# A top-k attention stage: max and min of the score halves read one half in PSUM; TensorE instead of VectorE spreads the reciprocal row sums

## The chip, the core and the metric

The kernel runs on one core of a Trainium2 chip. The metric is device time in microseconds of one execution; the three runs of the kernel before gave 1383.68, 1383.35 and 1379.19 us, median 1383.35.

## The reference

Three stages follow each other. Attention has 4 batches, 8 heads, 576 rows and head dimension 64, and keeps in each row of scores only those that reach the 32nd largest:

```
scores = scale * q @ k.T
kth    = 32nd largest of each row
scores = where(scores >= kth, scores, -1e9);  scores -= row max
attn   = exp(scores);  attn /= sum(attn) + 1e-9;  out = attn @ v
```

Then every one of the 2304 tokens goes through `h = x @ w_in; g = h * cos(h); y = g @ w_out` (512 to 2048 to 512), and at last through one of eight experts (512 to 1024 to 512) that a gate picks by argmax, scaled by the gate and by a sigmoid.

## The kernel before, in words

The program describes each piece of work as an operation with an engine, an estimated duration, the buffers that it reads and writes and a priority. A planner (class Plan) then runs a list schedule: at each moment each engine takes the most urgent operation that can start, where a buffer's place must be free too. The instructions are issued in the order that comes out, and each engine executes its own queue strictly in that order. The estimates never appear on the chip; they only fix the order.

Attention is cut into 80 units: 64 "main" units (128 rows of queries, for two heads) and 16 "mixed" ones (the last 64 rows of two heads, stacked). Unit u has priorities around 10*u. One main unit does this:

- TensorE multiplies q by k: for each head j two matmuls of 288 columns, L551, into four PSUM banks (mixed units: L566). Head 0 stands on partitions 0 to 63 and head 1 on 64 to 127.
- ScalarE copies each of the four results from PSUM to the SBUF tile sc (L557, mixed L571), which frees the bank.
- VectorE takes the elementwise max ("up") and min ("dn") of the left and the right half of each row, L580: four instructions of 288 columns per main unit, two per mixed one, both inputs in SBUF. Rounds of MAX8 (L585, L590, L600) and MATCH_REPLACE8 (L595) then find the 32nd and 33rd largest.
- GpSimd turns the threshold into a bias (L604, L607, L609), ScalarE computes a mask from sc (L614), GpSimd subtracts it (L618), ScalarE takes the exponential with row sums (L621), GpSimd adds 1e-9 (L624).
- VectorE takes the reciprocal (L627) and then copies it, repeated over 64 columns per head, into a 128x128 tile rs (L629). TensorE transposes the weights (L641, L652) and rs (L653), ScalarE copies these out of PSUM (L644, L657), TensorE multiplies by v (L682), and VectorE scales the result by the transposed reciprocals (L688, mixed L692).

Scores have priority offset -13.9 and the max and min 4.5, so the scores of a unit are due almost two units ahead of its max and min.

Six of the eight PSUM banks are shared by everything that TensorE writes (tag "ps"): transposed q and k, scores, transposed weights, results, and the first matmul of the dense stage. The other two accumulate the dense stage's second matmul. In the trace all banks have the one name bank.

Beside attention the same queues carry the conversion of the float64 weights to two single-precision parts (VectorE L714, L716, L729; GpSimd L725, L727, L739, L749), and the dense stage for each two finished tiles of tokens (TensorE L765 to L767 and L816 to L818; VectorE L775, L795; GpSimd L773, L777, L808). Routing and the eight experts follow when attention is over. All this lies in one order per engine: whatever waits holds up what is queued behind it on its engine.

Of the kernel before, what the change touches and what calls it, by code (L numbers as in the profile page):

```python
# [14 lines left out]
OP = mybir.AluOpType  # L15
AX = mybir.AxisListType

P = 128
# [10 lines left out]
UP_POOL = 0  # L29
ADD = {'q': -10.1,  # L30
 's': -13.9,
# [23 lines left out]
 'rs': 1,  # L55
# [13 lines left out]
class Buf:  # L69
    """A value in one of the places of its tag; the place is picked when the first op starts."""  # L70
# [16 lines left out]
class Plan:  # L87
    """Orders the ops of all engines: takes them in program order, finds what depends on what,
    and gives each engine the most urgent op that can start."""
# [9 lines left out]
    def tag(self, name, places, loose=False, under=None):  # L99
        """`places`: (ap, area, first, last) each; `under`: tags whose last values must have left the place."""  # L100
# [154 lines left out]
def act(n, extra=0, psum=False):  # L255
    return (49.0 + n * 0.837 if psum else 92.0 + n * 0.836) + 93.0 * extra
# [11 lines left out]
def tile_topk_attention_moe_moe2(ctx, tc, q, k, v, w_in, w_out, w_gate, w_ogate, w1, w2, out):  # L268
# [68 lines left out]
    def x2_rows(j):  # L337
        kind, b, r = tiles[j]
        if kind == "m":
# [5 lines left out]
              + N["dn"] * HALF + N["bl"] * S + 9 * P + (N["qt"] + N["rs"] + N["xt"]) * P + 4 * (TOPK + 16) + 32  # L345
# [73 lines left out]
    cut.tag("rs", N["rs"], P)  # L419
# [6 lines left out]
    attn_tags = ("sc", "kt", "qr", "vr", "kr", "ptm", "ptx", "up", "dn", "bl", "qx", "vx", "kx", "qt", "rs", "xt", "mx",  # L426
# [99 lines left out]
    def attention(u):  # L526
# [18 lines left out]
        for c in range(2):  # L545
            if kind == "m":
                ps = [plan.buf("ps"), plan.buf("ps")]
                for j in range(2):
                    def mm(j=j, c=c, o=ps[j]):
                        at = (REM if j == 0 else 0) + c * HALF  # L550
                        nc.tensor.matmul(o.ap[:, 0:HALF], qt.ap[j * D:(j + 1) * D, :],  # L551
                                         kt.ap[j * D:(j + 1) * D, at:at + HALF], start=True, stop=True)

                    plan.op({"PE": 483.0}, mm, [qt, kt], [ps[j]], prio + ADD["s"], hold=[sc])
                for j in range(2):
                    plan.op({"ACT": act(HALF, psum=True)},
                            lambda j=j, c=c, o=ps[j]: nc.scalar.activation(  # L557
                                sc.ap[:, j, c * HALF:(c + 1) * HALF], o.ap[:, 0:HALF], AF.Copy),
                            [ps[j]], [(sc, j)], prio + ADD["s"])
            else:  # L560
                o = plan.buf("ps")

                def mm(c=c, o=o):
                    at = REM + c * HALF
                    for j in range(2):
                        nc.tensor.matmul(o.ap[j * D:(j + 1) * D, 0:HALF], qt.ap[j * D:(j + 1) * D, 0:REM],  # L566
                                         kt.ap[j * D:(j + 1) * D, at:at + HALF], start=True, stop=True)

                plan.op({"PE": 540.0}, mm, [qt, kt], [o], prio + ADD["s"], hold=[sc])
                plan.op({"ACT": act(HALF, psum=True)},  # L570
                        lambda c=c, o=o: nc.scalar.activation(sc.ap[:, 0, c * HALF:(c + 1) * HALF],  # L571
                                                              o.ap[:, 0:HALF], AF.Copy),
                        [o], [(sc, 0)], prio + ADD["s"])

# [814 lines left out]
```

## Time and profile before

| what | value |
|---|---|
| median of three runs | 1383.35 us |
| span of the profiled execution, first to last instruction | 1382.2 us |
| TensorE busy | 1180.1 us (85%) |
| VectorE busy | 988.5 us (72%) |
| GpSimd busy | 885.2 us (64%) |
| ScalarE busy | 854.9 us (62%) |

The profile lists no time of its own for the profiled execution beside its span of 1382.2 us, which is 1.2 us under the median of the runs. The shares are averages over stretches that differ: attention and the dense stage fill the first 1000 us, the end of the dense stage, routing and experts the rest. A group's busy time is the union of its instructions, which can overlap their neighbour by some 0.08 us; the mean, minimum and median durations count each whole. In the trace one single-precision matmul has two MATMUL records, a transpose has one, and a few records are missing.

### The profile page before, as it was taken

What the parts mean: (1) busy time and instruction counts of PE and PEld (TensorE: products, weight loads), DVE (VectorE), ACT (ScalarE), POOL (GpSimd) and SP (SyncE); (2) the same over time, 40 slices, a digit from 0 to 9 for tenths busy, and PEclk for the clock granted to TensorE, in tenths of its full rate; (3) what the DMA queues carried; (4) which work ended last, traced back from release to release, by engine and by line L of the source; (5) the groups of instructions that cost most, each with busy time, mean ns of one, the idle gap of its engine ahead of it and who ended that gap; (6) DMA issues with size and microseconds to landing.
All of it is one profiled execution on the core that took longest, in us unless ns stands there. A gap on an engine that the chain in (4) does not pass through costs nothing.

```text
span 1382.2 us, 22655 instructions
## 1 busy us (share of the span) xinstructions
PE 1180.1 (85%) x7478; PEld 936.6 (68%) x7479; DVE 988.5 (72%) x2864; ACT 854.9 (62%) x1854; POOL 885.2 (64%) x1130
## 2 busy tenths in 40 slices
PE   3467778768898999999989898899994599999996
PEld 2334555547677668668767676767883599999995
DVE  6999999779599888999987889888335234444410
ACT  5777777767577787777766668767555244444421
POOL 6778888888666865776676657766765455555400
PEclk9655779989999989999999999999996699999998
DMA  8223323534440343323345321241557444444100
GB/s 210 76 107 113 98 67 116 182 131 162 144 139 8 111 140 105 122 92 104 96 135 152 100 78 36 89 137 46 174 184 267 166 160 158 149 156 160 58 17 23
DMA packets 95807, 164.72 MB, mean 119 GB/s; under 512 B 49850, under 2 KB 54202, under 8 KB 95680
## 3 DMA queue, kind: packets, MB, share of 16 engines
q1 hardware_dynamic: 91264, 153.71, 34.3%
q0 software_dynamic: 4416, 9.47, 2.1%
q8 instruction: 61, 1.00, 0.3%
q14 instruction: 66, 0.54, 0.1%
HBM read 146.72 MB, written 19.56 MB: 120 GB/s over the span
## 4 chain that ended last, share of the span: by engine, by line
PE 41%; DVE 29%; POOL 13%; issue 10%; ACT 6%; DMA 2%; POOLq 0%; DVEq 0%; ACTq 0%
DVE area_a L590 7%; DVE area_a L595 6%; DVE area_a L580 6%; PE bank L682 4%; PE bank L551 3%; PE bank L816 3%; PE bank L818 3%; PE bank L817 3%; PE bank L1052 2%; PE bank L1053 2%; PE bank L641 2%; PE bank L1054 2%; POOL area_a L618 2%; PE bank L765 2%; POOL area_g L777 2%
## 5 line engine op out<-in xcount | busy, mean ns | idle before, releaser
L590 DVE MAX8 area_a<-area_a 128x8 f32<-128x288 f32 x576 | 243.6, 444 | 1.1
L618 POOL TENSOR_TENSOR area_a<-area_a 128x576 f32<-128x576 f32 x144 | 195.8, 1368 | 23.0 <-ACT area_a L614 21.9
L595 DVE MATCH_REPLACE8 area_a<-area_a 128x288 f32<-128x288 f32 x432 | 187.8, 438 | 0.0
L580 DVE TENSOR_TENSOR area_a<-area_a 128x288 f32<-128x288 f32 x288 | 176.7, 639 | 14.5 <-ACT area_a L557 11.0
L765 PE MATMUL bank<-area_f,area_w 128*128 128x256 f32 x576 | 177.6, 308 | 2.3 <-ACT area_h L771 2.3
L641 PE MATMUL bank<-ident,area_a 128*128 128x128 f32 x576 | 104.5, 313 | 70.6 <-ACT area_a L621 57.8
L766 PE MATMUL bank<-area_f,area_w 128*128 128x256 f32 x576 | 163.3, 284 | 0.0
L767 PE MATMUL bank<-area_f,area_w 128*128 128x256 f32 x576 | 163.0, 283 | 0.0
L551 PE MATMUL bank<-area_a 64*128 64x288 f32 x512 | 133.3, 513 | 25.5 <-ACT area_a L541 22.5
L641 PEld LDWEIGHTS bank<-ident,area_a 128*128 128x128 f32 x576 | 73.8, 158 | 100.3 <-ACT area_a L621 78.4
L816 PE MATMUL bank<-area_l,area_f 128*128 128x512 f32 x288 | 130.4, 453 | 1.3 <-ACT area_f L806 0.6
L614 ACT ACTIVATE area_a<-area_a 128x576 bf16<-128x576 f32 x144 | 107.3, 768 | 37.5 <-POOL area_a L604 37.2
L808 POOL TENSOR_TENSOR area_f<-area_g,area_f 128x256 fp32r<-128x256 f32 x144 | 114.9, 811 | 23.7 <-ACT area_f L806 20.8
L777 POOL TENSOR_TENSOR area_g<-area_g,area_n 128x512 f32<-128x512 f32 x72 | 105.7, 1468 | 35.3 <-DVE area_a L600 14.8
L621 ACT ACTIVATE area_a<-area_a 128x576 f32<-128x576 f32 x144 | 111.2, 773 | 27.1 <-POOL area_a L618 26.2
L682 PE MATMUL bank<-area_a 128*64 128x128 f32 (+3 forms) x1600 | 123.3, 296 | 1.5 <-ACT area_a L662 1.3
L818 PE MATMUL bank<-area_l,area_f 128*128 128x512 f32 x288 | 119.7, 416 | 5.3 <-POOL area_f L808 5.0
L765 PEld LDWEIGHTS bank<-area_f,area_w 128*128 128x128 f32 x576 | 112.1, 195 | 14.2 <-issue 9.2
L682 PEld LDWEIGHTS bank<-area_a 128*64 128x64 f32 (+1 forms) x1600 | 89.8, 150 | 42.3 <-issue 18.3
L817 PE MATMUL bank<-area_l,area_f 128*128 128x512 f32 x288 | 118.2, 410 | 0.0
L766 PEld LDWEIGHTS bank<-area_f,area_w 128*128 128x128 f32 x576 | 111.8, 194 | 1.0
L767 PEld LDWEIGHTS bank<-area_f,area_w 128*128 128x128 f32 x576 | 111.0, 193 | 0.0
(197 smaller groups left out, 3005.4 us busy)
## 6 DMA issues: line engine op xcount, KB each, us to landing
area_l<-wod SPq DMA_DIRECT2D x144, 512.0 KB, 3.6
area_l<-in_moe_w_dram SPq DMA_DIRECT2D x52, 512.0 KB, 4.3
area_l<-in_moe_w_in_dram SPq DMA_DIRECT2D x16, 512.0 KB, 4.3
area_l<-in_moe_w_out_dram SPq DMA_DIRECT2D x16, 512.0 KB, 4.1
wod<-area_l SPq DMA_DIRECT2D x16, 512.0 KB, 2.6
area_n<-in_moe_w_dram SPq DMA_DIRECT2D x12, 512.0 KB, 4.9
area_a<-in_k_dram SPq DMA_DIRECT2D x32, 128.0 KB, 3.5
area_a<-in_q_dram SPq DMA_DIRECT2D x32, 128.0 KB, 3.4
```

The source lines that it names most:

```text
L551: nc.tensor.matmul(o.ap[:, 0:HALF], qt.ap[j * D:(j + 1) * D, :], kt.ap[j * D:(j + 1) * D, at:at + HALF], start=True, stop=True)
L580: plan.op(cost, lambda j=j, to=to, op=op, eng=eng: eng.tensor_tensor(to(), sc.ap[:, j, 0:HALF], sc.ap[:, j, HALF:S], op=op), [(sc, j)], [( ...
L590: lambda j=j, t=t: nc.vector.max(mx.ap[:, j, 8 * t:8 * t + 8], up.ap[:, j, :]),
L595: lambda j=j, t=t: nc.vector.match_replace(up.ap[:, j, :], mx.ap[:, j, 8 * t:8 * t + 8], up.ap[:, j, :], LOWEST),
L618: plan.op({"POOL": 1234.0}, lambda j=j: nc.gpsimd.tensor_tensor(sc.ap[:, j, :], sc.ap[:, j, :], bl.ap[:, j, :], op=OP.subtract), [(bl, j)] ...
L641: nc.tensor.transpose(pp.ap[:, r_ * P:(r_ + 1) * P], flat[:, at + r_ * P:at + (r_ + 1) * P], ident)
L682: nc.tensor.matmul(o.ap[j * D:(j + 1) * D, 0:w], lh, rh, start=(r_ == 0), stop=(r_ == R))
L765: nc.tensor.matmul(o, w_in_h[:, c_, fs], xh[:, c_, :], start=(c_ == 0), stop=False)
L766: nc.tensor.matmul(o, w_in_h[:, c_, fs], xl[:, c_, :], start=False, stop=False)
L767: nc.tensor.matmul(o, w_in_l[:, c_, fs], xh[:, c_, :], start=False, stop=(c_ == KC - 1))
L816: nc.tensor.matmul(acc[t].ap, gh, wr(0), start=(f == 0), stop=False)
L818: nc.tensor.matmul(acc[t].ap, gl, wr(0), start=False, stop=(f == NF - 1))
```

## The change

The matmuls of a unit now fill the right half ("high") first and then the left half ("low"), each as one operation of two matmuls for the two heads. ScalarE copies only the high half to SBUF ahead of the max and min (L560 of the new kernel). VectorE's max and min (L566 there) read the low half in its PSUM bank and the high half in SBUF. ScalarE's copy of the low half (L574 there) has a later priority offset, 4.0 in place of -13.9; the mask still needs both halves in SBUF. A low bank is free only when both the max and the min and this copy have read it. Dependences on sc are now kept by head and half.

The tile rs and VectorE's copy into it are gone. In their place TensorE multiplies the column of reciprocals, taken as a 64-column (mixed units: 128-column) operand by a stride of zero, by the identity: two matmuls per main unit (L641 there), one per mixed unit, in place of one transpose. The estimates change too: 620 ns for two score matmuls in place of 483 ns for each, 330 ns in place of 215 ns for the last transposes. Other priorities are as they were.

```diff
 ADD = {'q': -10.1,
+ 'low': 4.0,
...
-        for c in range(2):
-            if kind == "m":
-                ps = [plan.buf("ps"), plan.buf("ps")]
-                for j in range(2):
...
-                    plan.op({"PE": 483.0}, mm, [qt, kt], [ps[j]], prio + ADD["s"], hold=[sc])
...
+        low = [plan.buf("ps") for _ in range(n)]
+        high = [plan.buf("ps") for _ in range(n)]
+
+        def scores(c, out):
...
+        plan.op({"PE": 620.0}, lambda: scores(1, high), [qt, kt], high, prio + ADD["s"], hold=[sc])
+        plan.op({"PE": 620.0}, lambda: scores(0, low), [qt, kt], low, prio + ADD["s"], hold=[sc])
+        for j in range(n):
+            plan.op({"ACT": act(HALF, psum=True)}, lambda j=j: nc.scalar.activation(
+                sc.ap[:, j, HALF:S], high[j].ap[:, 0:HALF], AF.Copy), [high[j]], [(sc, (j, 1))], prio + ADD["s"])
...
-                plan.op(cost, lambda j=j, to=to, op=op, eng=eng: eng.tensor_tensor(
-                    to(), sc.ap[:, j, 0:HALF], sc.ap[:, j, HALF:S], op=op),
-                    [(sc, j)], [(up, j) if o_ else dns[j]], prio + ADD["top"])
+                plan.op({"DVE": vec(HALF)}, lambda j=j, to=to, op=op: nc.vector.tensor_tensor(
+                    to(), low[j].ap[:, 0:HALF], sc.ap[:, j, HALF:S], op=op),
+                    [low[j], (sc, (j, 1))], [(up, j) if o_ else dns[j]], prio + ADD["top"])
...
+        for j in range(n):
+            plan.op({"ACT": act(HALF, psum=True)}, lambda j=j: nc.scalar.activation(
+                sc.ap[:, j, 0:HALF], low[j].ap[:, 0:HALF], AF.Copy), [low[j]], [(sc, (j, 0))], prio + ADD["low"])
...
-        plan.op({"DVE": 136.0}, lambda: nc.vector.tensor_copy(
-            rs.ap.rearrange("p (h d) -> p h d", h=n),
-            sm.ap[:, 6:6 + n, None].to_broadcast([P, n, P // n])), [(sm, 6)], [rs], prio + ADD["sum"])
...
-            nc.tensor.transpose(px.ap[:, P:2 * P], rs.ap, ident)
-
-        plan.op({"PE": 215.0}, tx, [sc, rs], [px], prio + ADD["pt"], hold=[s2])
+            for j in range(n):
+                w_ = P // n
+                nc.tensor.matmul(px.ap[j * w_:(j + 1) * w_, P:2 * P], sm.ap[:, 6 + j:7 + j].to_broadcast([P, w_]), ident,
+                                 start=True, stop=True)
+
+        plan.op({"PE": 330.0}, tx, [sc, (sm, 6)], [px], prio + ADD["pt"], hold=[s2])
```

On TensorE the planner's order moves. This is a stretch of the early part before (bank numbers stand behind the name; L652 and L653 are the last transposes of one unit, L682 its product with v, L551 scores of a later unit):

```order
L652 MATMUL bank_114<-ident,area_a 128x128
L653 MATMUL bank_114<-ident,area_a 128x128 [waits DVE_49]
L551 MATMUL bank_119<-area_a 128x288
L682 MATMUL bank_116<-area_a 64x128
L682 MATMUL bank_116<-area_a 64x128 [waits Activation_49]
L682 MATMUL bank_116<-area_a 64x128 x6
L682 MATMUL bank_116<-area_a 64x128 [waits Activation_49]
L682 MATMUL bank_116<-area_a 64x128
L551 MATMUL bank_115<-area_a 128x288
L551 MATMUL bank_118<-area_a 128x288
L551 MATMUL bank_117<-area_a 128x288
```

Now, at the same place (L638 and L641 in the roles of L652 and L653, L671 in that of L682):

```order
L638 MATMUL bank_114<-ident,area_a 128x128
L641 MATMUL bank_114<-ident,area_a 64x128 [waits DVE_49]
L641 MATMUL bank_114<-ident,area_a 64x128
L671 MATMUL bank_115<-area_a 64x128 [waits Activation_49]
L671 MATMUL bank_115<-area_a 64x128 x7
L671 MATMUL bank_115<-area_a 64x128 [waits Activation_49]
L671 MATMUL bank_115<-area_a 64x128
L551 MATMUL bank_114<-area_a 128x288
L551 MATMUL bank_115<-area_a 128x288 [waits DVE_49]
L551 MATMUL bank_116<-area_a 128x288 [waits DVE_49]
L551 MATMUL bank_117<-area_a 128x288 [waits DVE_49]
```

Score matmuls no longer stand alone: over the whole program the 256 of the main units stood in 49 runs of one, 43 of two, 19 of three and 16 of four, and stand now in 58 runs of two and 35 of four. In exchange 81 of their rows wait for VectorE where 23 did.

On VectorE, a unit's max and min before (the reciprocal and the copy belong to the unit ahead):

```order
L580 TENSOR_TENSOR area_a<-area_a 128x288 x3
L590 MAX area_a<-area_a 128x8 [waits DVE_49,Pool_49]
L627 RECIPROCAL area_a<-area_a 128x2 [waits Pool_49]
L585 MAX area_a<-area_a 128x8 [waits DVE_49]
L629 COPY area_a<-area_a 128x128 [waits DVE_49]
L590 MAX area_a<-area_a 128x8
```

and now:

```order
L566 TENSOR_TENSOR area_a<-bank_117,area_a 128x288 [waits Activation_49]
L566 TENSOR_TENSOR area_a<-bank_118,area_a 128x288 [waits Activation_49]
L566 TENSOR_TENSOR area_a<-bank_117,area_a 128x288
L579 MAX area_a<-area_a 128x8 [waits DVE_49,Pool_49]
L571 MAX area_a<-area_a 128x8 [waits DVE_49,Pool_49]
L579 MAX area_a<-area_a 128x8
L566 TENSOR_TENSOR area_a<-bank_118,area_a 128x288 [waits DVE_49]
```

The order of the steps is kept, the copy is gone, and the instructions take their first input from a bank.

On ScalarE the copies of the low half (L574) stand behind VectorE's work in the new order; behind them here are the dense stage's L795 and the next steps of attention:

```order
L610 ACTIVATE area_a<-area_a 128x576 [waits Pool_49]
L574 ACTIVATE area_a<-bank_119 128x288 [waits DVE_49]
L574 ACTIVATE area_a<-bank_117 128x288 [waits DVE_49]
L795 ACTIVATE area_f<-area_g 128x256
L691 ACTIVATE area_f<-area_a 128x128 [waits DVE_49]
```

44 of the 144 low copies carry such a wait.

## Rows read from the trace of the kernel before

**Rows 1.** Windows: stretch, busy us per engine, granted clock, DMA share, GB/s.

```profile
0.00:250.00 250.00, 163.41 (x876) 110.82 (x878) 227.88 (x615) 177.18 (x394) 193.79 (x243) 0.75 0.38 114
250.00:1000.00 750.00, 682.51 (x4869) 526.33 (x4869) 628.81 (x2063) 531.91 (x1240) 518.87 (x725) 0.95 0.35 112
1000.00:1382.00 382.00, 334.21 (x1736) 299.49 (x1734) 131.84 (x186) 145.81 (x222) 172.49 (x164) 0.93 0.40 136
```

**Rows 2.** Chain of waits that ended last, shares by line: 0 to 250, 250 to 1000.

```profile
by line: DVE area_a L580 14.4%; DVE area_a L590 13.7%; DVE area_a L595 11.7%; PE bank L682 7.0%; DVE area_n L729 5.0%; DVE area_g L714 4.5%; DVE area_h L716 4.5%; issue 3.9%; DVE area_a L585 3.3%; DVE area_a L629 3.0%; POOL area_a L618 2.8%
...
by line: DVE area_a L590 7.9%; DVE area_a L595 6.9%; DVE area_a L580 5.9%; PE bank L682 5.5%; PE bank L816 4.8%; PE bank L551 4.7%; PE bank L818 4.2%; PE bank L641 4.2%; PE bank L817 4.1%; issue 4.0%; POOL area_g L777 3.3%; POOL area_a L618
```

**Rows 3.** Instructions of one line, whole run: duration min/median/max in ns.

```profile
L580 DVE TENSOR_TENSOR area_a<-area_a x288: 428/448/1557, 12.5 to 965.1; 128x288 f32<-128x288 f32 x144
...
L688 DVE TENSOR_TENSOR area_a<-bank,area_a x64: 264/283/293, 41.7 to 982.2; 128x128 f32<-128x128 f32 x64
...
L1035 DVE TENSOR_TENSOR area_f<-bank,area_f x24: 680/691/693, 1085.8 to 1331.3; 128x512 fp32r<-128x512 f32 x24
...
L629 DVE COPY area_a<-area_a x80: 199/219/1285, 37.3 to 979.0; 128x128 f32<-128x128 f32 x80
...
L777 POOL TENSOR_TENSOR area_g<-area_g,area_n x72: 1262/1288/2904, 162.7 to 1034.1; 128x512 f32<-128x512 f32 x72
```

**Rows 4.** Timeline, GpSimd and VectorE, two places: start us, us, instruction.

```profile
89.31 1.36 POOL L727 TENSOR_TENSOR area_n<-area_n,area_h 128x512 f32<-128x512 f32 x1
...
89.47 1.52 DVE L580 TENSOR_TENSOR area_a<-area_a 128x288 f32<-128x288 f32 x1
...
430.81 1.17 DVE L580 TENSOR_TENSOR area_a<-area_a 128x288 f32<-128x288 f32 x3
...
430.95 2.17 POOL L777 TENSOR_TENSOR area_g<-area_g,area_n 128x512 f32<-128x512 f32 x1 [3.52 <-DVE area_a L600]
```

**Rows 5.** Windows of L580, then of L629: VectorE busy us, instructions, clock.

```profile
0.00:250.00 250.00, 52.13 (x70) 0.75 0.38 114
250.00:1000.00 750.00, 124.58 (x218) 0.95 0.35 112
...
0.00:250.00 250.00, 8.68 (x15) 0.75 0.38 114
250.00:1000.00 750.00, 25.16 (x65) 0.95 0.35 112
```

**Rows 6.** TensorE's waits, first 0 to 250, then 250 to 1000: us, times, longest.

```profile
PE bank L653 <- DVE area_a L629: 18.6, 12, 3.5
...
PE bank L641 <- ACT area_a L621: 34.8, 26, 7.1
PE bank L653 <- DVE area_a L629: 14.9, 15, 2.5
```

**Rows 7.** Timeline, VectorE and TensorE around one copy.

```profile
91.29 0.14 DVE L627 RECIPROCAL area_a<-area_a 128x2 f32<-128x2 f32 x1
...
91.71 1.06 DVE L629 COPY area_a<-area_a 128x128 f32<-128x128 f32 x1
...
92.83 0.47 PE L653 MATMUL bank<-ident,area_a 128*128 128x128 f32 x1 [2.67 <-DVE area_a L629]
```

**Rows 8.** Timeline, TensorE at the full clock (records, two to a matmul).

```profile
454.84 1.46 PE L682 MATMUL bank<-area_a 128*64 128x128 f32 x20
456.23 0.75 PE L551 MATMUL bank<-area_a 64*128 64x288 f32 x2
456.91 0.66 PE L641 MATMUL bank<-ident,area_a 128*128 128x128 f32 x4
457.49 0.76 PE L551 MATMUL bank<-area_a 64*128 64x288 f32 x4
458.18 0.66 PE L641 MATMUL bank<-ident,area_a 128*128 128x128 f32 x4
...
464.24 1.24 PE L551 MATMUL bank<-area_a 64*128 64x288 f32 x8
465.41 0.50 PE L816 MATMUL bank<-area_l,area_f 128*128 128x512 f32 x1
...
460.25 0.27 PE L652 MATMUL bank<-ident,area_a 128*128 128x128 f32 x1
460.36 0.27 PE L653 MATMUL bank<-ident,area_a 128*128 128x128 f32 x1
```

More of the change, by code (lines that the diff above doesn't have):

```diff
@@ L54 @@
  'qt': 2,
- 'rs': 1,
  'xt': 2,
@@ L425, in tile_topk_attention_moe_moe2 @@
     plan.op({"POOL": 200.0}, lambda: nc.gpsimd.memset(flags, -1.0), [], [B_flags], -1000.0)
[L426 removed]
+    attn_tags = ("sc", "kt", "qr", "vr", "kr", "ptm", "ptx", "up", "dn", "bl", "qx", "vx", "kx", "qt", "xt", "mx",
                  "sm")
@@ L544, in attention @@
         sc = plan.buf("sc")
-        for c in range(2):
-            if kind == "m":
-                ps = [plan.buf("ps"), plan.buf("ps")]
-                for j in range(2):
[L549 to L552, printed above, removed]
-                    plan.op({"PE": 483.0}, mm, [qt, kt], [ps[j]], prio + ADD["s"], hold=[sc])
[L555 to L573, printed above, removed]
@@ new lines, in attention @@
+        low = [plan.buf("ps") for _ in range(n)]
+        high = [plan.buf("ps") for _ in range(n)]
+        def scores(c, out):
+            at = REM + c * HALF
+            for j in range(2):
+                if kind == "m":
+                    lo = at if j == 0 else at - REM
+                    nc.tensor.matmul(out[j].ap[:, 0:HALF], qt.ap[j * D:(j + 1) * D, :],
+                                     kt.ap[j * D:(j + 1) * D, lo:lo + HALF], start=True, stop=True)
+                else:
+                    nc.tensor.matmul(out[0].ap[j * D:(j + 1) * D, 0:HALF], qt.ap[j * D:(j + 1) * D, 0:REM],
+                                     kt.ap[j * D:(j + 1) * D, at:at + HALF], start=True, stop=True)
@@ L615, in attention @@
                 bl.ap[:, j, :], sc.ap[:, j, :], AF.Relu, scale=-MASK_GAIN, bias=sm.ap[:, 2 + j:3 + j]),
-                [(sc, j), (sm, 2)], [(bl, j)], prio + ADD["mask"])
+                [(sc, (j, 0)), (sc, (j, 1)), (sm, 2)], [(bl, j)], prio + ADD["mask"])
         for j in range(n):
             plan.op({"POOL": 1234.0}, lambda j=j: nc.gpsimd.tensor_tensor(
-                sc.ap[:, j, :], sc.ap[:, j, :], bl.ap[:, j, :], op=OP.subtract), [(bl, j)], [(sc, j)], prio + ADD["sub"])
+                sc.ap[:, j, :], sc.ap[:, j, :], bl.ap[:, j, :], op=OP.subtract), [(bl, j)], [(sc, (j, 0)), (sc, (j, 1))], prio + ADD["sub"])
         for j in range(n):
@@ L622, in attention @@
                 sc.ap[:, j, :], sc.ap[:, j, :], AF.Exp, scale=scale, bias=sm.ap[:, j:j + 1],
-                accum_out=sm.ap[:, 4 + j:5 + j]), [(sm, 0)], [(sc, j), (sm, 4)], prio + ADD["exp"], kind="exp")
+                accum_out=sm.ap[:, 4 + j:5 + j]), [(sm, 0)], [(sc, (j, 0)), (sc, (j, 1)), (sm, 4)], prio + ADD["exp"],
+                kind="exp")
         plan.op({"POOL": 160.0}, lambda: nc.gpsimd.tensor_scalar(
             sm.ap[:, 6:6 + n], sm.ap[:, 4:4 + n], 1.0, 1e-9, op0=OP.mult, op1=OP.add), [(sm, 4)], [(sm, 6)], prio + ADD["exp"])
-        rs = plan.buf("rs")
         plan.op({"DVE": 80.0}, lambda: nc.vector.reciprocal(sm.ap[:, 6:6 + n], sm.ap[:, 6:6 + n]),
                 [], [(sm, 6)], prio + ADD["sum"])
-        plan.op({"DVE": 136.0}, lambda: nc.vector.tensor_copy(
-            rs.ap.rearrange("p (h d) -> p h d", h=n),
-            sm.ap[:, 6:6 + n, None].to_broadcast([P, n, P // n])), [(sm, 6)], [rs], prio + ADD["sum"])
         ptm = []
@@ L641, in tp @@
                     nc.tensor.transpose(pp.ap[:, r_ * P:(r_ + 1) * P], flat[:, at + r_ * P:at + (r_ + 1) * P], ident)
-            plan.op({"PE": 430.0}, tp, [(sc, j)], [pp], prio + ADD["pt"], hold=[s1])
+            plan.op({"PE": 430.0}, tp, [(sc, (j, 0)), (sc, (j, 1))], [pp], prio + ADD["pt"], hold=[s1])
             plan.op({"ACT": act(512, psum=True)}, lambda pp=pp, s1=s1: nc.scalar.activation(
```

5 lines of the change are left out of this document (1 added, 4 removed).

## The prediction, made before the changed kernel ran

> **What bounds the kernel now.** I read the windows first, to see which engine is full in which stretch. In the first 250 us VectorE is busy for 227.88 us (91%), GpSimd for 193.79 (78%) and TensorE for 163.41 (65%) [rows 1]. From 250 to 1000 us TensorE is busy for 682.51 of 750 us (91%), VectorE for 628.81 (84%) [rows 1]. After 1000 us attention is over, and nothing that the change touches runs. The chain of waits says the same by another way: in the early stretch the VectorE lines that it lists hold 14.4 + 13.7 + 11.7 + 5.0 + 4.5 + 4.5 + 3.3 + 3.0 = 60% of it, and the max and min, L580, lead; in the later one the three listed VectorE lines hold 7.9 + 6.9 + 5.9 = 21%, and TensorE's many lines the most [rows 2]. So a microsecond of VectorE should be worth about 0.6 us early and 0.2 us late, and what TensorE executes counts late nearly in full.
>
> Next I looked at single instructions of the lines that change. L580 has a minimum of 428 and a median of 448 ns but a maximum of 1557 [rows 3]. The timeline shows why: at 89.47 one takes 1.52 us, begun 0.16 us after a GpSimd instruction of 1.36 us, and it ends 0.3 us after that one; at 430.95 it is GpSimd that takes 2.17 us, begun behind three L580 [rows 4], where its line's median is 1288 ns [rows 3]. The two engines hold each other up where VectorE reads two SBUF inputs. VectorE instructions whose first input is in PSUM don't show it: L688 lies between 264 and 293 ns, L1035 between 680 and 693 [rows 3].
>
> **Part 1: max and min with one input in PSUM.** No instruction of 288 columns with that form is in the trace. L688 has 128 columns and a median of 283 ns, L1035 512 and 691 [rows 3]: 408 ns for 384 columns, 1.06 ns each, so 288 columns should take 283 + 160 x 1.06 = 453 ns. Bounds: 283 ns below and 691 above; I take 453, between two rows of the same kind. Before, the 70 instructions of the early stretch are busy for 52.13 us (0.745 each) and the 218 later ones for 124.58 (0.571) [rows 5]. At 0.453 that is 31.7 and 98.8: VectorE is relieved of 20.4 us early and 25.8 us late. GpSimd is relieved where it was the one held up; I count nothing for it.
>
> L688 and L1035 leave no room for a PSUM price beside L580's undisturbed 448 ns [rows 3]. [...]
>
> **Part 2: the copy L629 goes.** Its busy time is 8.68 us early and 25.16 us late [rows 5], all of it removed. The wait behind it changes too: TensorE's last transpose waited for it for 18.6 us in 12 times early and 14.9 us in 15 times late [rows 6]. Now it waits for the reciprocal, which is also VectorE's. Around 92 us the reciprocal ends at 91.43 and the copy at 92.77, and TensorE had waited for 2.67 us [rows 7]: half of the wait remains. Late I take 7 of 14.9 us (bounds 0 and 14.9); early this lies beside VectorE's own time and gives nothing more.
>
> VectorE's relief is 29.1 us early (20.4 + 8.7) and, without the copy, 25.8 us late. With the shares of the chain: early 29.1 x 0.6 = 18 us (bounds 0 and 29), late 25.8 x 0.21 = 5 us (bounds 0 and 25.8).
>
> **Part 3: TensorE's extra matmuls.** The ten matmuls of L682 take 1.39 us from 454.84 to the next start, 0.14 each, and a transpose 0.11 (460.25 to 460.36) [rows 8]. Two such matmuls in place of one transpose cost 0.17 us in each of 64 main units, one costs 0.03 in 16 mixed ones: 11.4 us. By L580's counts [rows 5] 218/288 = 0.757 of this falls late, where TensorE is full: +9 us. An operand read with a stride of zero is not in the trace. Below, both together cost as little as the transpose (0); above, they cost as much as a pair of score matmuls (0.69, next part): 0.58 x 64 + 0.23 x 16 = 41 us, +31 late. I take L682, which has the same 64-column form.
>
> **Part 4: the order of the score matmuls.** A score matmul alone, at 456.23, takes 0.68 us until the next start; two neighbours, at 457.49, take 0.69 together, and four, at 464.24, 1.17 [rows 8]: those of the two heads stand on different partitions and run side by side. The order has 49 single ones, 43 twos and 35 threes or fours before, and 58 twos and 35 fours after. Three cost about as much as four. Before: 49 x 0.68 + 43 x 0.69 + 35 x 1.17 = 104 us; after: 58 x 0.69 + 35 x 1.17 = 81. That is 23 us less, 17 of it late. Where a wait for a bank parts a pair, it doesn't hold; the bounds are 0 and 17.
>
> **Part 5: banks.** A low bank stays taken until VectorE has read it twice. This is the price that I cost at nothing. What hides it is the cover on VectorE: behind its max and min a unit has its MAX8 and MATCH_REPLACE8 rounds, seven per head, during which the next scores can be written. If that cover is gone, the second rival comes. ScalarE's copies are as many as before, at ScalarE 71% busy in both stretches [rows 1]; behind them in its queue wait the exponentials' successors, so a late low copy delays the mask of its own unit first.
>
> **Sum.** Early -18. Late +9 - 17 for TensorE's work, -7 for the wait on the copy, -5 for VectorE: -20. Against the span of 1382.2 us, which is 1.2 us below the median of the runs, the changed kernel takes 1344 us, and 1346 as a median.
>
> **The rivals.**
> - *More comes through.* If VectorE sets the whole early stretch, all 29 us count; late, all of the 14.9 us go and half of TensorE's 34.8 us of waits for the exponentials [rows 6], since that chain starts at VectorE, with the 8 us of TensorE's work: 29 + 15 + 17 + 8 = 69, so 1314. For it speaks VectorE's 91%, against it that chains through GpSimd and ScalarE keep their lengths.
> - *Banks become the bound, and it gets slower.* Score rows that wait for VectorE go from 23 to 81. TensorE executes in order, so a score matmul that waits for the bank of an older unit's min or result holds up the dense stage behind it. The nearest price is that of the wait on the copy: 18.6 + 14.9 = 33.5 us in 27 times, 1.24 us each [rows 6]. 0.757 x 58 = 44 late rows of that price are 55 us, and 1346 + 55 = 1401. It decides from 37/44 = 0.84 us per wait. For it speaks that most of the new waits stand right behind one another; against it that VectorE gets lighter and that a wait in the order need not be one in time. [...]
> - *The relief is taken up again.* GpSimd is 78% busy early [rows 1], and other VectorE instructions with two SBUF inputs or long GpSimd neighbours may be held up in place of L580. Then early only the copy counts, 8.7 x 0.6 = 5 us, and late the 8 us of TensorE's work: 1371. If reading zero-stride operands costs more, this comes out at no change.
>
> **How the numbers follow.** Forecast 0.53, more comes through 0.12, taken up again 0.20, banks 0.15. A difference under 0.3%, about 4 us, can't be told from no change; I give the third case 0.04 of that and the banks 0.02. Faster is 0.53 + 0.12 + 0.16 = 0.81, same 0.06, slower 0.13. The range leaves out half of the first rival and nearly all of the banks' case: 1320 to 1380.
>
> **What would show it.** Right: the new max and min at 440 to 470 ns with hardly any above 500; VectorE's total some 80 us below 988; GpSimd's longest L777 shorter; the early stretch ahead by 15 to 25 us at the same unit; scores in pairs, with the line's busy time down by some 20 us; no single wait of score matmuls for VectorE above some 20 us in sum. Wrong: waits of score matmuls for VectorE of 40 us or more late; the new max and min at 550 ns or more; or VectorE relieved as said and the end of attention where it was.

## The result, and the profile after

The changed kernel takes 1324.47 us (median of four runs, 1323.0 to 1324.81); the kernel before took 1381.27 beside it on the same chip (1378.81 to 1383.68). The ratio is 0.9587, 95% interval 0.957 to 0.9603: 57 us less, where 38 were forecast. The time lies in the forecast's range, 1320 to 1380, 22 us below its value.

To see where the 57 us are, both traces are cut at the same work and not at the same time: at the 16th and at the last of the 64 results of main units that VectorE scales (L688 before, L677 after). Read on a grid of half a us, the 16th has begun by 254.5 us before and by 233.0 after; the last begins at 982.2 [rows 3] and at 925.8. What lies ahead of the 16th is called early here, what lies between the two points late. These are the windows of the kernel before between those points (stretch and its length, busy us of TensorE, its weight loads, VectorE, ScalarE and GpSimd, granted clock, DMA share, GB/s):

```profile
0.00:254.50 254.50, 167.91 (x916) 114.84 (x917) 230.29 (x619) 179.36 (x399) 197.81 (x246) 0.75 0.37 113
254.50:982.20 727.70, 660.21 (x4717) 506.19 (x4717) 623.40 (x2054) 524.42 (x1221) 505.35 (x710) 0.95 0.35 111
982.20:1382.20 400.00, 352.01 (x1848) 315.62 (x1848) 134.84 (x192) 151.12 (x235) 182.00 (x176) 0.93 0.41 139
```

And of the kernel after:

```profile
0.00:233.00 233.00, 162.31 (x958) 110.03 (x960) 209.33 (x590) 178.91 (x396) 190.63 (x246) 0.79 0.41 123
233.00:925.80 692.80, 647.01 (x4889) 504.23 (x4889) 581.25 (x2004) 520.08 (x1222) 468.50 (x709) 0.96 0.38 117
925.80:1322.40 396.60, 348.98 (x1842) 312.80 (x1841) 134.50 (x192) 152.63 (x236) 181.31 (x175) 0.93 0.41 139
```

The early stretch is 21.5 us shorter (18 forecast), the later one 34.9 (727.7 - 692.8; 20 forecast), what follows attention 3.4. Late, VectorE lost 42 us of busy time and GpSimd 37, though the change takes no instruction from GpSimd. TensorE's busy time fell by 13 us and its idle time from 727.7 - 660.2 = 67.5 us to 692.8 - 647.0 = 45.8.

The lines that changed, over the whole run, in the kernel after (min/median/max in ns; first and last start):

```profile
L566 DVE TENSOR_TENSOR area_a<-bank,area_a x288: 423/444/459, 11.5 to 909.0; 128x288 f32<-128x288 f32 x144
...
L677 DVE TENSOR_TENSOR area_a<-bank,area_a x64: 264/291/294, 44.2 to 925.8; 128x128 f32<-128x128 f32 x64
...
L766 POOL TENSOR_TENSOR area_g<-area_g,area_n x72: 1258/1282/1797, 145.2 to 976.3; 128x512 f32<-128x512 f32 x72
...
L705 DVE TENSOR_SCALAR area_h<-area_l x32: 402/585/1511, 5.3 to 301.6; 128x512 int32<-128x512 int32 x32
```

L566, the max and min with one input in PSUM, never goes above 459 ns; as L580 it went up to 1557 [rows 3]. GpSimd's subtraction of the dense stage, now L766, has a longest of 1797 ns, not 2904 [rows 3]. But L705, a conversion of the dense stage's weights with one SBUF input, takes the place of the max and min in part. Here it is in the kernel before:

```profile
L716 DVE TENSOR_SCALAR area_h<-area_l x32: 402/416/1522, 5.5 to 324.0; 128x512 int32<-128x512 int32 x32
```

Its median went from 416 to 585 ns. One of them, of 1.50 us, begins 0.17 us behind a GpSimd instruction and ends 0.3 us after it, as L580 did in [rows 4]:

```profile
56.29 1.38 POOL L728 TENSOR_TENSOR area_w<-area_n,area_w 128x512 fp32r<-128x512 f32 x1 [1.12 <-ACT area_w L726]
...
56.46 1.50 DVE L705 TENSOR_SCALAR area_h<-area_l 128x512 int32<-128x512 int32 x1
```

The groups of VectorE in the early stretch show the size, before (to 255 us) and then after (to 235 us; busy us, mean ns):

```profile
L729 DVE SCALAR_TENSOR_TENSOR area_n<-area_l,area_n 128x512 int32<-128x512 int32 x26 | 23.9, 918 | 4.6 <-POOL area_n L727 4.6
L716 DVE TENSOR_SCALAR area_h<-area_l 128x512 int32<-128x512 int32 x27 | 17.1, 632 | 0.0
```

```profile
L566 DVE TENSOR_TENSOR area_a<-bank,area_a 128x288 f32<-128x288 f32 x69 | 28.5, 441 | 0.5 <-PE bank L551 0.5
L718 DVE SCALAR_TENSOR_TENSOR area_n<-area_l,area_n 128x512 int32<-128x512 int32 x26 | 28.2, 1085 | 6.8 <-POOL area_n L716 6.8
L705 DVE TENSOR_SCALAR area_h<-area_l 128x512 int32<-128x512 int32 x27 | 24.1, 893 | 0.0
```

The max and min and the copy together fell by 23.6 + 9.8 = 33 us to the 16th unit (52.13 to 28.5, and 16 copies of 0.612 us), but these two lines rose by 4.3 + 7.0 = 11. By the windows above VectorE is relieved by 21 us early (230.3 to 209.3), not by 29.

TensorE's waits over the whole run, after (us, times, longest):

```profile
PE bank L627 <- ACT area_a L610: 32.2, 18, 8.7
...
PE bank L627 <- ACT area_a L560: 11.9, 7, 3.9
...
PE bank L641 <- DVE area_a L616: 8.0, 9, 2.1
...
PE bank L754 <- ACT area_a L560: 5.0, 2, 3.8
...
PE bank L551 <- DVE area_a L566: 3.8, 4, 2.6
...
PE bank L551 <- DVE area_a L677: 2.7, 4, 1.2
```

And before:

```profile
PE bank L641 <- ACT area_a L621: 57.8, 44, 7.1
PE bank L653 <- DVE area_a L629: 33.5, 27, 3.5
...
PE bank L641 <- ACT area_a L557: 10.5, 2, 9.9
```

The waits for the exponentials (L610, L621 before) and for what spreads the row sums (L616, L629 before) fell from 91.3 to 40.2 us together. A score matmul waits for VectorE in eight cases, 6.5 us in sum: these new bank dependences cost little. Another wait for banks grew: for ScalarE's copies of the high halves (L560) TensorE waited 16.9 us in nine cases, where it waited 10.5 us in two for the copies of the scores before (L557); 12.6 of the 16.9 lie in the later stretch, none of the 10.5. L754, a matmul of the dense stage, reads nothing that L560 writes, so it waits there for a bank. The chain of waits that ended last changed its owner; its shares by engine, before and then after:

```profile
PE 41%; DVE 29%; POOL 13%; issue 10%; ACT 6%; DMA 2%; POOLq 0%; DVEq 0%; ACTq 0%
```

```profile
PE 65%; DVE 12%; POOL 8%; ACT 8%; issue 4%; DMA 2%; SPq 0%; ACTq 0%; POOLq 0%; DVEq 0%
```

### The profile page after: what moved, and what is told of

Read it like the earlier page. It is cut to its first block, busy times and chain, and to the rows that moved or that the text cites. A ratio compares the mean times of both kernels' runs of the same rounds, so it can differ in the third digit from the quotient of the medians.

```text
span 1322.4 us, 23058 instructions
## 1 busy us (share of the span) xinstructions
PE 1158.3 (88%) x7686; PEld 927.1 (70%) x7687; DVE 925.1 (70%) x2784; ACT 851.6 (64%) x1854; POOL 840.4 (64%) x1130
## 4 chain that ended last, share of the span: by engine, by line
PE 65%; DVE 12%; POOL 8%; ACT 8%; issue 4%; DMA 2%; SPq 0%; ACTq 0%; POOLq 0%; DVEq 0%
PE bank L671 6%; PE bank L551 5%; PE bank L754 5%; PE bank L805 4%; PE bank L627 4%; PE bank L756 4%; PE bank L755 4%; PE bank L807 4%; PE bank L806 4%; PE bank L1041 4%; PE bank L1042 3%; PE bank L1043 3%; PE bank L1061 3%; PE bank L1060 3%; PE bank L1059 3%
## 5 line engine op out<-in xcount | busy, mean ns | idle before, releaser
L607 POOL TENSOR_TENSOR area_a<-area_a 128x576 f32<-128x576 f32 x144 | 190.6, 1332 | 30.1 <-ACT area_a L603 28.7
L754 PE MATMUL bank<-area_f,area_w 128*128 128x256 f32 x576 | 179.0, 311 | 7.7 <-ACT area_a L560 5.0
L627 PE MATMUL bank<-ident,area_a 128*128 128x128 f32 x576 | 99.3, 303 | 51.0 <-ACT area_a L610 32.2
L566 DVE TENSOR_TENSOR area_a<-bank,area_a 128x288 f32<-128x288 f32 x288 | 120.0, 444 | 17.8 <-ACT area_a L574 6.7
L754 PEld LDWEIGHTS bank<-area_f,area_w 128*128 128x128 f32 x576 | 112.6, 195 | 26.8 <-issue 13.3
L805 PE MATMUL bank<-area_l,area_f 128*128 128x512 f32 x288 | 128.2, 445 | 2.5 <-ACT area_f L795 1.3
L551 PE MATMUL bank<-area_a 64*128 64x288 f32 x512 | 109.8, 489 | 20.4 <-ACT area_a L539 10.9
L610 ACT ACTIVATE area_a<-area_a 128x576 f32<-128x576 f32 x144 | 111.5, 774 | 18.2 <-POOL area_a L607 17.4
L797 POOL TENSOR_TENSOR area_f<-area_g,area_f 128x256 fp32r<-128x256 f32 x144 | 113.8, 805 | 12.6 <-ACT area_f L795 10.6
L671 PE MATMUL bank<-area_a 128*64 128x128 f32 (+3 forms) x1600 | 115.8, 284 | 4.4 <-ACT area_a L650 1.9
L807 PE MATMUL bank<-area_l,area_f 128*128 128x512 f32 x288 | 116.7, 405 | 2.8 <-POOL area_f L797 2.5
L806 PE MATMUL bank<-area_l,area_f 128*128 128x512 f32 x288 | 115.9, 402 | 0.0
L755 PEld LDWEIGHTS bank<-area_f,area_w 128*128 128x128 f32 x576 | 113.3, 197 | 1.4
L671 PEld LDWEIGHTS bank<-area_a 128*64 128x64 f32 (+1 forms) x1600 | 84.9, 143 | 39.4 <-issue 18.9
L756 PEld LDWEIGHTS bank<-area_f,area_w 128*128 128x128 f32 x576 | 112.4, 195 | 0.0
L766 POOL TENSOR_TENSOR area_g<-area_g,area_n 128x512 f32<-128x512 f32 x72 | 95.0, 1320 | 26.7 <-DVE area_a L589 11.8
```

Of the source, the lines that this page charges most:

```text
L551: nc.tensor.matmul(out[j].ap[:, 0:HALF], qt.ap[j * D:(j + 1) * D, :], kt.ap[j * D:(j + 1) * D, lo:lo + HALF], start=True, stop=True)
L607: plan.op({"POOL": 1234.0}, lambda j=j: nc.gpsimd.tensor_tensor(sc.ap[:, j, :], sc.ap[:, j, :], bl.ap[:, j, :], op=OP.subtract), [(bl, j)] ...
L627: nc.tensor.transpose(pp.ap[:, r_ * P:(r_ + 1) * P], flat[:, at + r_ * P:at + (r_ + 1) * P], ident)
L671: nc.tensor.matmul(o.ap[j * D:(j + 1) * D, 0:w], lh, rh, start=(r_ == 0), stop=(r_ == R))
L754: nc.tensor.matmul(o, w_in_h[:, c_, fs], xh[:, c_, :], start=(c_ == 0), stop=False)
L755: nc.tensor.matmul(o, w_in_h[:, c_, fs], xl[:, c_, :], start=False, stop=False)
```

## The experiments

### One part at a time

Of the change, e1 has only the max and min that read PSUM (with the high half first and the late low copies that belong to them), with the score matmuls one by one and VectorE's copy kept; e2 only the score matmuls in pairs; e3 only the spread on TensorE.

```diff
 e1, against the kernel after
-        plan.op({"PE": 620.0}, lambda: scores(1, high), [qt, kt], high, ...)
-        plan.op({"PE": 620.0}, lambda: scores(0, low), [qt, kt], low, ...)
+        for c, out in ((1, high), (0, low)):
+            for j in range(2):
+                plan.op({"PE": 483.0}, lambda ...: scores(c, out, (j,)), [qt, kt], [out[j]], ...)
+        plan.op({"DVE": 136.0}, lambda: nc.vector.tensor_copy(rs..., sm...), ...)
-                nc.tensor.matmul(px..., sm.ap[:, 6 + j:7 + j].to_broadcast([P, w_]), ident, ...)
+            nc.tensor.transpose(px.ap[:, P:2 * P], rs.ap, ident)
 e2, against the kernel before
-                    plan.op({"PE": 483.0}, mm, [qt, kt], [ps[j]], prio + ADD["s"], hold=[sc])
+                plan.op({"PE": 620.0}, mm, [qt, kt], ps, prio + ADD["s"], hold=[sc])
 e3, against the kernel before
-            nc.tensor.transpose(px.ap[:, P:2 * P], rs.ap, ident)
+            for j in range(n):
+                nc.tensor.matmul(px..., sm.ap[:, 6 + j:7 + j].to_broadcast([P, w_]), ident, ...)
```

> Only the max and min read the low half in PSUM (low copy later); single score matmuls and VectorE's copy of the reciprocals as before. Theory A (the forecast's terms add up, VectorE's relief worth 0.6 early and 0.2 late): about -17 us, near 1365, TensorE's late waits for the exponentials still 30 us or more. Theory B (the late gain comes from VectorE no longer running behind, which brings the exponentials in time): -30 to -40 us, near 1347, those late waits halved. Theory C (it is the new order, whatever its reason): anywhere between -15 and +15.

> Only the two score matmuls of a half become one operation of the two heads (620 ns in the planner); everything else as before. Theory A: TensorE's busy time of the score line down by 20 us or more, time -14 to -18 us, near 1366. Theory B: the same work saved, but part of it turns into longer waits for the exponentials, since VectorE still runs behind: -5 to -10 us. Theory C: -15 to +15.

> Only TensorE spreads the reciprocals and VectorE's copy is gone; scores and max and min as before. Theories A and B: -3 us (-5 early, -7 of waits for the copy, +9 of TensorE work late), between -10 and +3; the late waits of the last transpose fall from 15 us to about 7. Theory C: -15 to +15.

| run | median, us | ratio to before (95%) | 16th unit begun by, last begins at |
|---|---|---|---|
| e1, PSUM alone | 1328.96 | 0.9625 (0.9602 to 0.9649) | 234.5, 929.4 |
| e2, pairs alone | 1365.54 | 0.9898 (0.9871 to 0.9925) | 249.0, 965.1 |
| e3, spread alone | 1385.93 | 1.0038 (1.0017 to 1.0058) | 247.5, 987.2 |

Against their 1380.38 of before that is -51, -15 and +6: the sum, -60, is about the whole, though on top of e1 the pairs give 19 and the spread takes 14 (e5 below). e1 gained more than any of its three theories had said (B's sign, late waits for the exponentials halved, came true: 34.8 to 15.9 us), and e3 lost more than A and B allowed. The gain is the PSUM part's, 20 us of it early and 727.7 - 694.9 = 33 late. Its windows and its waits:

```profile
0.00:234.50 234.50, 169.78 (x914) 115.64 (x916) 209.41 (x606) 179.12 (x397) 189.29 (x246) 0.72 0.41 123
234.50:929.40 694.90, 644.18 (x4707) 500.60 (x4706) 599.20 (x2066) 520.54 (x1220) 463.48 (x707) 0.97 0.36 116
```

```profile
PE bank L639 <- ACT area_a L617: 28.2, 24, 6.5
...
PE bank L651 <- DVE area_a L627: 15.3, 15, 3.4
```

Late, VectorE is busy for 24 us less and GpSimd for 42. TensorE's idle time falls from 67.5 to 50.7 us, and its busy time by 16 us with nearly the same matmuls (10 of 4717 records fewer, some 3 or 4 us of the 16): the granted clock is 0.97 where it was 0.95, and busy time times clock is nearly unchanged (660.2 x 0.95 = 627, 644.2 x 0.97 = 625). So about half of the late gain is TensorE waiting less, and most of the rest TensorE at a higher granted clock in this execution. That the shorter waits brought the higher clock isn't shown. e3 waited less than the kernel before, too (739.7 - 685.0 = 54.7 us), at 0.94:

```profile
247.50:987.20 739.70, 685.02 (x4892) 519.44 (x4892) 625.78 (x2005) 524.29 (x1223) 495.19 (x711) 0.94 0.35 111
```

The four executions of e1 had mean clocks from 0.910 to 0.938 at times only 5 us apart. The waits for the exponentials and the copy fall by 91.3 - 43.5 = 48 us although the copy is still there.

e3 shows something more. The copy that it takes off VectorE was busy for 33.8 us (8.68 + 25.16, [rows 5]), but VectorE's whole busy time fell by 3.4 us only, from 988.5 to 985.1. Its other lines took 20 us more, above all max and min (180.9 us for 176.7), the dense stage's L774 (39.2 for the 33.1 of L775) and the three conversions of the weights (77.7 for 71.4); the remaining 10 us are overlap, since neighbours overlap by some 0.08 us and a line's busy time is more than what it adds to its engine's. So as long as max and min read two SBUF inputs, most of the copy's relief was taken up again. From e5 to e10 (below), where they don't, the copy's 39.6 us went, VectorE's busy time fell by 27.8, and its other lines took 1 us more.

### Is it the order that the planner makes of other estimates?

e4 is the kernel before with nothing changed but two numbers of the planner, max and min at 560 ns and the copy at 350.

```diff
-                eng, cost = (...) if u < UP_POOL else (nc.vector, {"DVE": vec(HALF)})
+                eng, cost = (...) if u < UP_POOL else (nc.vector, {"DVE": 560.0})
-        plan.op({"DVE": 136.0}, lambda: nc.vector.tensor_copy(
+        plan.op({"DVE": 350.0}, lambda: nc.vector.tensor_copy(
```

> The kernel before with the planner's estimates of the max and min (369 to 560 ns) and of the reciprocal copy (136 to 350 ns) set near what the trace of before shows; no instruction differs, only the order. Theories A and B: within 8 us of before, since VectorE has the same work and is held up the same. Theory C (a plan from truer estimates is what gains): -15 us or more.

1385.77 us, ratio 1.004 (1.002 to 1.006): 5 us more. Another order made by truer numbers doesn't give the gain; that theory falls for these numbers. No run has the order of e1 with both inputs of max and min in SBUF, so what e1's own order adds or takes isn't measured by itself; the prices of the next section leave little for it in the later stretch, but not in the early one.

### What a microsecond of VectorE and of GpSimd is worth

The forecast had taken 0.21 for VectorE late, from the chain, and nothing for GpSimd. In the kernel after, e6 has each MAX8 of the minima twice (144 more), e7 four tiny memsets on GpSimd behind each subtraction (576 more); both leave what is computed as it is.

```diff
-                            lambda j=j: nc.vector.max(mx..., dns[j].ap),
+                            lambda j=j: [nc.vector.max(mx..., dns[j].ap) for _ in range(2)],
...
-            plan.op({"POOL": 1234.0}, lambda j=j: nc.gpsimd.tensor_tensor(sc..., bl..., op=OP.subtract), ...)
+            plan.op({"POOL": 1234.0}, lambda j=j: [nc.gpsimd.tensor_tensor(sc..., bl..., op=OP.subtract),
+                *[nc.gpsimd.memset(spacer, 0.0) for _ in range(4)]], ...)
```

> The changed kernel with the first MAX8 behind each min done twice: 144 more VectorE instructions of 288 columns with one SBUF input, about 0.37 us each, 53 us in all, which is what the max and min got shorter by; the planner's estimates and the order are the same. Theory V (VectorE's own time is what the change gives): 30 to 50 us of the 57 come back, 1355 to 1375. Theory G (it is that the two engines no longer hold each other up, GpSimd's 45 us above all): 5 to 20 us, 1330 to 1345.

> The changed kernel with four tiny GpSimd memsets of one element behind each subtraction of the mask, about 0.09 us each and some 50 us in all, about the 45 us that GpSimd's busy time fell by; estimates and order the same. They read no SBUF. Theory V: 0 to 15 us slower, up to 1340. Theory G: 25 to 45 us slower, 1350 to 1370.

e6 took 1355.57 us (0.9806, 0.9776 to 0.9836), 31 more than the kernel after; e7 1345.7 (0.9735, 0.9708 to 0.9763), 21 more. The first is what V had said; the second lies between V and G, so both engines' time counts. Windows of the doubled MAX8, first in the kernel after, then in e6 (VectorE busy us, instructions, clock):

```profile
0.00:233.00 233.00, 15.06 (x34) 0.79 0.41 123
233.00:925.80 692.80, 49.16 (x110) 0.96 0.38 117
```

```profile
0.00:236.50 236.50, 30.86 (x68) 0.76 0.40 121
236.50:956.20 719.70, 100.16 (x220) 0.96 0.36 113
```

Late it added 51 us, and the later stretch is 719.7 - 692.8 = 26.9 us longer: 26.9/51 = 0.53 us per us (0.59 by VectorE's whole late busy time, which rose by 45). The memsets in e7:

```profile
0.00:235.50 235.50, 13.24 (x128) 0.78 0.40 121
235.50:946.50 711.00, 40.93 (x448) 0.96 0.36 114
```

They added 40.9 us late, and the later stretch is 711.0 - 692.8 = 18.2 us longer: 18.2/40.9 = 0.44 (0.56 by GpSimd's whole late busy time, which rose by only 32, from 468.5 to 500.8). With the lower two rates the late relief of e1 is worth 24.2 x 0.53 + 41.9 x 0.44 = 13 + 18 = 31 us, with the higher two, which are in the same terms as the relief, 14 + 23 = 38; 33 were measured. By either more than half of it is GpSimd's, which was counted at nothing. The rates come from work added to the faster kernel; that they hold for work taken from the slower one is borne out by the sum alone.

### The banks

e8 is the kernel after with five score banks where it has six; e11 gives the low halves' copies a more urgent priority, so that they can free their banks sooner.

```diff
-    plan.tag("ps", banks[0:6], loose=True)
+    plan.tag("ps", banks[0:5], loose=True)
...
- 'low': 4.0,
+ 'low': -13.9,
```

> The changed kernel with five shared PSUM banks in place of six; the planner makes its own order for it. If the longer hold of the low banks costs as little as the forecast put it (nothing): within 10 us, up to 1335. If banks are nearly the bound (the slower rival, not far off): 30 us or more slower, above 1355, with waits of score matmuls for VectorE in the list.

> The changed kernel with ScalarE's low copies at the early priority of the scores (-13.9 in place of 4.0), so that only their place in the order moves. If the later low copies matter (ScalarE reaches the high copies and so VectorE its max and min earlier): 10 us or more slower than the changed kernel, above 1334. If all of the gain is in what VectorE and GpSimd no longer spend: within 6 us of 1324.

e8: 1328.12 us (0.961, 0.9574 to 0.9647); e11: 1328.98 (0.9626, 0.9586 to 0.9666). Their intervals overlap that of the kernel after. One bank less costs 4 us by the medians, and at most some 11 by the intervals (0.9647 - 0.957). In e11 the 16th unit has begun by 225.5 us, 7.5 earlier, but the later stretch takes 703.5 us, 10.7 more, so that nothing is gained. A bank more or less isn't what bounds this kernel, though TensorE's waits for ScalarE's copies, 16.9 us in nine cases in the kernel after, show that banks aren't free either.

### What the spread costs

e5 is the kernel after with VectorE's copy and the transpose in place of the spread. e9 is e5 with the transpose of the copy written three times (160 more), to price TensorE's time. e10 is e5 with ScalarE making the copy. e12 is e10 with 200 more transposes.

```diff
 e9, against e5
-            nc.tensor.transpose(px.ap[:, P:2 * P], rs.ap, ident)
+            for _ in range(3):
+                nc.tensor.transpose(px.ap[:, P:2 * P], rs.ap, ident)
 e10, against e5
-        plan.op({"DVE": 136.0}, lambda: nc.vector.tensor_copy(
+        plan.op({"ACT": act(P)}, lambda: nc.scalar.activation(
 e12, against e10
-            nc.tensor.transpose(px.ap[:, P:2 * P], rs.ap, ident)
+            for _ in range(3 + u % 2):
+                nc.tensor.transpose(px.ap[:, P:2 * P], rs.ap, ident)
```

> The changed kernel with VectorE's copy of the reciprocals and the transpose put back: max and min in PSUM and paired scores alone. If the parts add as measured one by one (-51, -15, +5 us): 5 us faster than the changed kernel, about 1318. If the copy's wait behind VectorE matters once the rest is gone (forecast's part 2): 1328 to 1335.

> The kernel of max and min in PSUM and paired scores (1310 us), with the transpose of the repeated reciprocals done three times into the same place: 160 more transposes of 0.11 us, 18 us of TensorE, nothing else, estimates and order the same. It stands beside the changed kernel, which pays 14 us for TensorE's spreading. If those 14 us are TensorE's work, which now sets the pace: +10 to +18. If they come from the other order or the wait for the reciprocal: +0 to +5.

> Max and min in PSUM and paired scores, with ScalarE making the repeated reciprocals in place of VectorE (ScalarE 65% busy, VectorE 72%): neither VectorE's 40 us nor TensorE's spreading. At 0.58 us per us of VectorE, as the filler on VectorE gave, up to 20 us faster than 1310; if ScalarE's queue is as late, no change; if every wait for ScalarE holds up TensorE, slower by 5 to 10.

> This kernel is e10 (ScalarE makes the copy of the reciprocal row sums; neither VectorE nor a TensorE spread is used for it), and each unit's transpose of that copy is written three or four times in place of once: 200 extra transposes, by e9's price (160 took 16.5 us of TensorE) about 20 us of TensorE, as much as the spread puts there (1158.3 against 1138.0 us). It tells apart why the spread costs 14.5 us more than psum_pairs although it also takes 27 us off VectorE, which e10 showed to be worth 14.5 us. Theory A (TensorE's time alone, once TensorE sets the pace the relief of VectorE is worth little): about 20 us of TensorE cost nearly their full length here, 1312 to 1318 us. Theory B (the two add up by e9's price of 10 us for 16.5): 1308 us, and the spread then has another cost of some 16 us, in where its matmuls stand or what they wait for.

| run | median, us | ratio to before (95%) | TensorE late: stretch, busy, idle |
|---|---|---|---|
| after | 1324.47 | 0.9587 (0.957 to 0.9603) | 692.8, 647.0, 45.8 |
| e5 | 1310.25 | 0.9477 (0.9444 to 0.951) | 679.8, 629.7, 50.1 |
| e9 | 1320.26 | 0.9554 (0.9517 to 0.9591) | 689.4, 642.2, 47.2 |
| e10 | 1295.78 | 0.9393 (0.9357 to 0.9429) | 667.8, 625.8, 42.0 |
| e12 | 1305.42 | 0.9455 (0.9409 to 0.95) | 680.5, 639.4, 41.1 |

The stretches run from the 16th main unit to the last; these are the rows of e5, e9, e10 and e12:

```profile
231.50:911.30 679.80, 629.67 (x4733) 493.35 (x4732) 598.21 (x2070) 523.29 (x1228) 469.55 (x711) 0.97 0.38 120
```

```profile
233.00:922.40 689.40, 642.17 (x4861) 508.20 (x4860) 601.40 (x2070) 524.58 (x1228) 466.68 (x710) 0.97 0.37 118
```

```profile
228.50:896.30 667.80, 625.77 (x4721) 494.26 (x4718) 570.52 (x1990) 532.47 (x1286) 464.20 (x709) 0.97 0.38 122
```

```profile
228.00:908.50 680.50, 639.42 (x4883) 508.76 (x4880) 572.13 (x1991) 533.48 (x1287) 466.35 (x710) 0.98 0.38 120
```

e5, with 1310.25 us, is faster than either of its expectations. Without the spread the kernel is 14 us faster. Late, the spread adds 17.3 us to TensorE's busy time and takes 4.3 off its idle time: +13.0. The fillers show that most of this busy time counts there: e9 has 12.5 us more busy for 9.6 us of time, e12 13.7 for 12.7. Over the whole run less comes out, 10 us each for 16.5 and 15.7 us of TensorE, so that theory B's figure was nearer for e12 than A's.

B's other cost of 16 us isn't settled. The kernel after is 28.7 us behind e10, with TensorE busy for 23.1 us more (1158.3 against 1135.2). By e12's price over the whole run TensorE's time is 14 of these 28.7; by its late price it is some 20 of the 25 us that the later stretch is longer (692.8 against 667.8). Some of the rest is VectorE's, which is 8 us busier than in e10 (925.1 against 916.8). Whether the spread has another cost, from where its matmuls stand or what they wait for, stays open. e10 shows what the copy's relief is worth when TensorE doesn't pay for it: 12.0 us late (idle 8.1 less, busy 3.9 less), 3 us early, 14.5 in all by the medians. It is the fastest version, 1295.78 us, faster than both kernels.

That the spread is dear is seen at one place, before and then after (start us, us):

```profile
439.62 0.27 PE L652 MATMUL bank<-ident,area_a 128*128 128x128 f32 x1
439.72 0.27 PE L653 MATMUL bank<-ident,area_a 128*128 128x128 f32 x1
439.75 0.36 PE L765 MATMUL bank<-area_f,area_w 128*128 128x256 f32 x1
```

```profile
400.46 0.27 PE L638 MATMUL bank<-ident,area_a 128*128 128x128 f32 x1
400.66 0.44 PE L641 MATMUL bank<-ident,area_a 128*64 128x128 f32 x4
401.03 0.39 PE L754 MATMUL bank<-area_f,area_w 128*128 128x256 f32 x1
```

From the last transpose of the weights to the next matmul it was 0.13 us and is 0.57. By these starts a main unit pays 0.44 us, 28 us for 64, where 0.17 was forecast. The whole busy time says 1158.3 - 1138.0 = 20 us, and it decides: the place shown before is a cheap one, as it was 0.31 us or more at the units behind which a score matmul follows.

## Why the prediction was right in sign and too small

- **The PSUM operand: right.** 453 ns forecast, 444 measured, and none above 459. A price for reading PSUM isn't seen: 444 ns stand beside L580's undisturbed 448 [rows 3].
- **The early 18 us: right by luck.** 21.5 were measured, 20.0 of them in e1 alone. VectorE was relieved by 21 us and not 29, as the conversions of the weights were held up in place of the max and min; that was the third rival, in part. In return each microsecond brought about one of time, not 0.6. The fillers don't bear that out: e6 lost 3.5 us for 15.8 of VectorE added early (30.86 - 15.06) and e7 2.5 for 13.2 of GpSimd. By these rates the early relief of e1, 20.9 us of VectorE and 8.5 of GpSimd, explains 6 of its 20 us; the rest stays open, and the new order may have a part in it.
- **The late relief: this step failed.** "late 25.8 x 0.21 = 5 us" by [rows 2], and of GpSimd "I count nothing for it". e1 gained 33 us late by this part alone, more than the upper bound of 25.8. VectorE's relief itself came out nearly as forecast, 24.2 us. Its rate did not: the 0.21 is VectorE's share of one chain through a stretch in which the engines pass the work on to each other, and e6 measured 0.53 to 0.59. GpSimd was relieved of 42 us late, and e7 prices that at 0.44 to 0.56. The rows were there: [rows 4] showed GpSimd held up, 2.17 us for a line whose median is 1.29, and [rows 3] its longest. The forecast also had no term for the granted clock, 0.97 late in e1 and 0.95 before, whose cause is open.
- **The wait on the copy: merged with the one before it.** 7 of 14.9 us were forecast late [rows 6]. In e1, with the copy kept, TensorE's wait for it fell from 33.5 to 15.3 us over the run and that for the exponentials from 57.8 to 28.2: so these waits hung on the chain that starts at VectorE more than on the copy. Late alone they fell from 14.9 to 8.5 and from 34.8 to 15.9. The first rival had named this: half of the waits for the exponentials go with VectorE's delay.
- **The pairs: right.** L551's busy time fell from 133.3 to 109.8 us, -23.5 for -23. Alone they gave 15 us of time, 11.6 of them late, and on top of e1 19, 15.1 of them late, where 17 were forecast.
- **The spread: the second step that failed.** 11.4 us of TensorE were forecast by L682's 0.14 per matmul; 20 were measured (21 in e3 alone, 1180.1 to 1201.2). The bound above, 41 us, held. With the copy gone the part was forecast a small gain (9 late for TensorE, against 7 late and 5 early); it is a loss of 14. Nor did all of the copy's time come off VectorE: its total fell by 63 us, not by the 80 that the prediction named as a sign.
- **The banks: nearly right at nothing.** The second rival needed 0.84 us for each of 44 waits for VectorE; eight waits took 6.5 us. The waits for ScalarE's high copies, 12.6 us late, were in no term. Whether ScalarE and VectorE lose time by reading one bank isn't shown: the durations of L566, 423 to 459 ns, and of the low copies L574, 387 to 447 where L557 took 384 to 467 before, show no price, but the two also wait for each other, L574 8.1 us in 16 cases and L566 6.7 us in 10.

Late, the sum had -5 for the relief, -17 for the pairs and 9 - 7 = +2 for the spread: -20. By e1, by e5 against e1 (679.8 - 694.9) and by the kernel after against e5 (692.8 - 679.8) it was -33, -15 and +13: -35. Two errors of unlike sign, 28 us too little gain for the relief and 11 too little cost for the spread, and 2 for the pairs leave 15 of the 22 us of span by which the forecast fell short; 3.5 are early, 3 after attention. That the time lies inside the range is in part owed to these errors going against each other. Two smaller sums are off by about a microsecond: by their own terms the forecast is 1345 and the third rival 1370.

## What to carry to other kernels

A share of the chain of waits is no exchange rate: here, with TensorE, VectorE, ScalarE and GpSimd busy for 93, 84, 75 and 68% of the late stretch and passing the work on, about half of what was added to VectorE or GpSimd came through late (0.53 and 0.44), and a filler on the engine in question measures that directly. When two engines hold each other up, the relief of the one that is not edited belongs into the sum: GpSimd's, counted at nothing here, was 42 us late in e1. Work that is moved from a full engine onto the one that becomes the bound has to be priced there: here the same copy cost 14 us less on ScalarE than on VectorE, and 14 us more on TensorE.

## What the runs showed of the hardware

- One SBUF input didn't always keep a VectorE instruction short beside GpSimd: L705 has one, and in the kernel after its 32 instructions lie at 402/585/1511 ns (the one of 1.50 us at 56.46 stands beside GpSimd's L728), the copy L629 at 199/219/1285 [rows 3]. The MAX8 of the minima, doubled in e6, stays at one duration:

```profile
L571 DVE MAX8 area_a<-area_a x288: 434/461/469, 12.6 to 940.5; 128x8 f32<-128x288 f32 x144
```

- As one line was relieved, others took longer: max and min lost 57 us of busy time over the run (176.7 [rows 5] to 120.0, 28.5 of these by 235 us) and the copy its 34, yet VectorE as a whole only 63 (988.5 to 925.1), 27 us less than that: other lines took 21 us more, the rest is overlap of neighbours. GpSimd lost 45 (885.2 to 840.4). In e3, where the copy alone goes, VectorE's other lines took 20 us more; the copy itself went from 33.8 us to 39.6 in e5, where max and min read PSUM.
- TensorE's granted clock, at 1.00 in 118 of the 145 stretches of 5 us from 255 to 980 us of the kernel before and at 0.50 in two, was 0.95 in the later stretch of the kernel before and 0.97 in e1, with nearly the same matmuls and with 67.5 and 50.7 us idle; in e3 it was 0.94 with 54.7 us idle. Idle time alone doesn't order these three, and what decides the clock within the stretch stays open.
- Two small single-precision matmuls whose one operand is read with a stride of zero took 0.37 us to the next start (400.66 to 401.03; 0.36 or 0.37 at 46 of 48 such places in the later stretch), where the ten of L682 take 0.14 each [rows 8].
